# Who turns q and k, who applies the mask, and in what order: three changes at once to a BigBird attention and Fourier-mixing kernel

## The chip, the cores and the metric

The kernel runs on one NeuronCore of a Trainium2 chip. Times are device microseconds (us) of that core, from the first instruction to the last; "ns" is written where nanoseconds are meant. The profile of a kernel is one of its executions, so its span can differ from the median by a few tenths of a per cent.

## The reference, cut to what matters

```python
# attention: batch 4, 8 heads, 768 positions, 64 features a head, blocks of 32 positions
scores = scale * np.matmul(q, k.transpose(0, 1, 3, 2))
mask = np.abs(blk_i - blk_j) <= 1                      # a window of blocks,
mask = mask | (blk_i == 0) | (blk_j == 0) | (blk_i == 23) | (blk_j == 23)   # the outer blocks,
...                                                    # and three random blocks a row
scores = np.where(mask, scores, -1e9)
attn = softmax(scores);  x = attn @ v                  # heads side by side: 768 x 512 a batch
# Fourier mixing and channels
u  = x + real(fft(fft(x, axis=1), axis=2))
un = (u - mean(u)) / np.sqrt(var(u) + 1e-6)
out = u + np.maximum(un @ w_ch1, 0) @ w_ch2            # 512 -> 2048 -> 512
```

All of it is fp32. The output must agree with the reference.

Of the kernel before, what the change touches and what calls it, by code (L numbers as in the profile page):

```python
# [11 lines left out]
FP32 = mybir.dt.float32  # L12
BF16 = mybir.dt.bfloat16
# [4 lines left out]
ALU = mybir.AluOpType  # L18
ACT = mybir.ActivationFunctionType
# [45 lines left out]
           ((384, 64, 191, 64, 64, -1), (704, -128, 64, 63, 63, -1), (640, 127, 0, 1, 1, 1)))  # L65


def _rows(view, tile):

    got = []  # L70
    for t, p0, runs, jump, n, s0, step in _ORDER:
        if t != tile:
            continue
        at = view[s0:s0 + 1, :]
        row, col = list(at.ap[0])[0], list(at.ap[1])
        if jump > 0:
            got.append((p0, runs * n, bass.AP(tensor=at.tensor, offset=at.offset,
                                              ap=[[jump * row, runs], [step * row, n], col])))
            continue
        for r in range(runs):  # L80
            at = view[s0 + r * jump:s0 + r * jump + 1, :]
            got.append((p0 + r * n, n, bass.AP(tensor=at.tensor, offset=at.offset,
                                               ap=[[step * row, n], col])))
    return got
# [3 lines left out]
def kernel(  # L88
# [32 lines left out]
    scale = 1.0 / float(D) ** 0.5  # L121
    KA = D + NB
    NP = H // 2
    LIMIT = 400.0

    const = ctx.enter_context(tc.tile_pool(name="const", bufs=1))

# [49 lines left out]
    def busy(engine, us, after=0.0):  # L177
        when[engine] = max(when[engine], after) + us
        return when[engine]
# [13 lines left out]
    pairs = [(b, j) for b in range(B) for j in range(NP)]  # L193
    loaded, v_of = {}, {}

    def load_k(n, queue=None):

        b, j = pairs[n]
        kt = loaded.get((n, 1))
        if kt is None:  # L200
            kt = ld.tile([P, C, 2, D], FP32, tag="k", name="kr")
        for i in range(2):
            (queue or nc.sync).dma_start(out=kt[:, :, i, :],
                                         in_=k[b, 2 * j + i].rearrange("(p c) d -> p c d", p=P))
        loaded[n, 1] = kt

    def load_q(n):

        b, j = pairs[n]
        qt = loaded.get((n, 0))  # L210
        if qt is None:
            qt = loaded[n, 0] = ld.tile([P, T, 2, 2, D], FP32, tag="q", name="qr")
        for t in range(T):
            for i in range(2):
                rows = q[b, 2 * j + i][2 * P * t:2 * P * (t + 1), :]
                nc.sync.dma_start(out=qt[:, t, :, i, :],
                                  in_=rows.rearrange("(p r) d -> p r d", r=2))
# [47 lines left out]
    def warm(n):  # L265

        m = ps_m.tile([P, P], FP32, tag="m", name="warm")
        for _ in range(n):
            nc.tensor.matmul(m, ident, ident, start=True, stop=True)
# [126 lines left out]
    def room(i, shape, name, dtype=FP32):  # L396
        return big.tile(shape, dtype, tag=f"big{i}", name=name)
# [29 lines left out]



    turned, e_of, acc_of, o_of, sums_of, x_of, sp_of = {}, {}, {}, {}, {}, {}, {}  # L430
    s_at, e_at, oT_at, acc_at = {}, {}, {}, {}

    def turn(n, a, half):

        t = loaded[n, a]
        if half == 0:
            turned[n, a] = tp_p.tile([P, S], FP32, tag="qk"[a] + "T", name="qk"[a] + "T")
        dst = turned[n, a]
        first = n == 0 and half == 0
        tag, pool = ("m", ps_m) if first and a == 0 else ("t", ps_t)  # L440
        tp, at = pool.tile([P, 512], FP32, tag=tag, name="tp"), bank(tag)
        if a == 0:
            parts = [t[:, c // 2, c % 2, :, :] for c in (range(4, 6) if half else range(4))]
        else:
            parts = [t[:, T * half + c, :, :] for c in range(T)]
        for c, part in enumerate(parts):
            nc.tensor.transpose(tp[:, c * P:(c + 1) * P], part, ident)  # L447
        done = busy("PE", 0.15 * len(parts)) + HOP
        if a == 1:
            nc.scalar.copy(out=dst[:, half * HS:(half + 1) * HS], in_=tp[:, 0:HS])  # L450
            give(at, busy("ACT", 0.5, done))
        else:
            for i, (to, to_jump, frm, jump, cnt, step) in enumerate(_TURNED[half]):
                on, copy = (("DVE", nc.vector.tensor_copy) if n == 0 and (half == 1 or i % 2 == 0)
                            else ("ACT", nc.scalar.copy))
                copy(out=_grid(dst, to, 2, to_jump, cnt, 1),
                     in_=_grid(tp, frm, 2, jump, cnt, step))
                end = busy(on, 0.27 if cnt > 1 else 0.18, done)
            give(at, end)
        if half == 1:  # L460
            flat = t.rearrange("p t r i d -> p (t r i d)" if a == 0 else "p c i d -> p (c i d)")
            nc.scalar.activation(out=flat, in_=flat, func=ACT.Square,
                                 accum_out=peaks[:, 2 * n + a:2 * n + a + 1])
            busy("ACT", 1.05)

    UP = 2 * C
    UNITS = len(pairs) * UP
    SLOT = 2

    def scores(u):  # L470
        n, w = divmod(u, UP)
        half, c = divmod(w, C)
        qT, kT = turned[n, 0], turned[n, 1]
        s = ps_s.tile([P, 2, 512], FP32, tag="s", name="s")
        busy("PE", 0.72 if n >= NP else 1.0, max(e_at.get(u - SLOT, 0.0), z_at[u % 2]))
        s_at[u] = when["PE"] + HOP
        for i in range(2):
            nc.tensor.matmul(s[:, i, 0:HS], kT[D * i:D * i + D, c * P:(c + 1) * P],  # L478
                             qT[D * i:D * i + D, half * HS:(half + 1) * HS],
                             start=True, stop=n >= NP)  # L480
        if n < NP:
            for i in range(2):
                nc.tensor.matmul(s[:, i, 0:HS], of_k[D * i:D * i + NB, c * P:(c + 1) * P],  # L483
                                 off_q[D * i:D * i + NB, half * HS:(half + 1) * HS],
                                 start=False, stop=True)
        return s

    def weigh(u, s):
        n, w = divmod(u, UP)
        half, c = divmod(w, C)  # L490
        e = ep.tile([P, 2, HS], FP32, tag="e", name="e")
        e_of[u] = e
        if n < NP:
            nc.scalar.activation(out=e, in_=s[:, :, 0:HS], func=ACT.Exp, scale=scale)
            e_at[u] = busy("ACT", 0.8, s_at[u]) + HOP
            return
        nc.scalar.activation(out=s[:, :, 0:HS], in_=s[:, :, 0:HS], func=ACT.Exp, scale=scale)  # L497
        m = mask[:, c, half * HS:(half + 1) * HS].rearrange("p (o s) -> p o s", o=1)
        nc.vector.tensor_tensor(out=e, in0=s[:, :, 0:HS], in1=m.broadcast_to([P, 2, HS]),  # L499
                                op=ALU.mult)  # L500
        e_at[u] = busy("DVE", 0.97, busy("ACT", 0.8, s_at[u]) + HOP) + HOP
        if c > 0:
            acc_at[n, half] = busy("POOL", 2.0, e_at[u]) + HOP
        if c == 1:
            acc_of[n, half] = acc_p.tile([P, 2, HS], FP32, tag="acc", name="acc")

        for i in range(2 if c > 0 else 0):
            acc = acc_of[n, half][:, i, :]
            nc.gpsimd.tensor_add(out=acc, in0=e_of[u - 1][:, i, :] if c == 1 else acc,  # L509
                                 in1=e[:, i, :])  # L510
# [646 lines left out]
    def begin(b):  # L1157


        before, after, rest = mixer(b, x_of[b, 0], x_of[b, 1])  # L1160
        any_of = len(late) + len(apart) + 4 * len(rest)
        hold = 2 * T
        apart.extend((*step, any_of) for step in norm_steps(b) + before)
        apart.extend((*step, hold) for step in after)
        apart.append(("-", lambda: late.extend(rest), 0.0, 0.0, 0.0, hold))

    def w_loads():
        while state["got"] < min(len(wchunks), state["w"] + ROOMS):
# [3 lines left out]
    def w_steps(sl):  # L1172
        while state["w"] < min(len(wchunks), W_PACE * sl):
            w_round(state["w"])
            state["w"] += 1

    def slot(sl):
# [35 lines left out]
            short.append(("t", acc_at[n - 1, 1], lambda: total(n - 1)))  # L1213
        if n + 1 < len(pairs):
            for at, a, half in ((1, 0, 0), (2, 0, 1), (4, 1, 0), (5, 1, 1)):
                if s == at:
                    short.append(("t", 0.0, lambda a=a, half=half: turn(n + 1, a, half)))
            if s == 1:
                load_v(n + 1)
# [15 lines left out]
            channel_step()  # L1235
            gap(max(state["owed"], 0.0))

        while short and (s in (2, 5) or len(short) > 1 or phase == 0 or sl == B * SB):
            short.popleft()[2]()
        if s == 3 and n + 2 < len(pairs):  # L1240
            load_q(n + 2)
        if s == 0 and 0 < n < len(pairs) - 1:
            load_k(n + 1)
        w_loads()
        w_steps(sl)
        if sl >= 4 and sl % 2 == 0:
            table_step()

# [20 lines left out]
    state["got"] = 2  # L1269
    turn(0, 1, 0)  # L1270
    turn(0, 0, 0)
    warm(3)
    spread_q(keep_q[0:NB, :], keep)
    w_loads()
    for sl in range(B * SB + 1):
# [112 lines left out]
```

## The kernel before: the parts that the change touches

Two heads make a pair, so there are 16 pairs in 4 batches. A **unit** is one block of 128 keys against half the queries (384), for the two heads of a pair: 12 units a pair, 192 in all. A **slot** is two units. In each slot TensorE makes the scores of two units, ScalarE exponentiates them, and TensorE multiplies the exponentials of the slot before with v. Around this, the generator deals out other work: Fourier mixing and channel products of earlier batches, and small tasks from a list called `short`. It places them by a model of its own, `when[engine]`, advanced by `busy(engine, us)`. The model decides the order in which instructions are written; the engines then work off their queues in that order.

The turn of q or k of a pair, in two halves each: six blocks of 128 x 128 are transposed on TensorE into PSUM, the memory that TensorE's products land in (here its bank `t`), and copied to `qT` or `kT` in SBUF, the core's working memory. q is copied into an order that suits the Fourier mixing, in several pieces:

```python
def turn(n, a, half):                       # pair n, a = 0 for q, 1 for k
    tp, at = pool.tile([P, 512], FP32, tag=tag, name="tp"), bank(tag)
    for c, part in enumerate(parts):
        nc.tensor.transpose(tp[:, c * P:(c + 1) * P], part, ident)
    if a == 1:
        nc.scalar.copy(out=dst[:, half * HS:(half + 1) * HS], in_=tp[:, 0:HS])
    else:
        for i, (to, to_jump, frm, jump, cnt, step) in enumerate(_TURNED[half]):
            on, copy = (("DVE", nc.vector.tensor_copy) if n == 0 and (half == 1 or i % 2 == 0)
                        else ("ACT", nc.scalar.copy))
            copy(out=_grid(dst, ...), in_=_grid(tp, ...))
    ...                                     # then ScalarE sums squares for a later check
```

The mask. In the first batch (`n < NP`, pairs 0 to 3) TensorE adds it to the scores as a product of two small bf16 factors, 24 rows deep. From the second batch on VectorE multiplies a 0/1 mask in after the exponential:

```python
def scores(u):
    for i in range(2):
        nc.tensor.matmul(s[:, i, 0:HS], kT[D*i:D*i+D, c*P:(c+1)*P], qT[...], start=True, stop=n >= NP)
    if n < NP:
        for i in range(2):
            nc.tensor.matmul(s[:, i, 0:HS], of_k[...], off_q[...], start=False, stop=True)

def weigh(u, s):
    if n < NP:
        nc.scalar.activation(out=e, in_=s[:, :, 0:HS], func=ACT.Exp, scale=scale)
        return
    nc.scalar.activation(out=s[:, :, 0:HS], in_=s[:, :, 0:HS], func=ACT.Exp, scale=scale)
    nc.vector.tensor_tensor(out=e, in0=s[:, :, 0:HS], in1=m.broadcast_to([P, 2, HS]), op=ALU.mult)
    ...                                     # GpSimd adds e to a running sum
```

The small tasks of a slot are taken strictly in the order in which they were listed. After them come the loads of weights and their rounding on ScalarE and VectorE (`w_steps`):

```python
        while short and (s in (2, 5) or len(short) > 1 or phase == 0 or sl == B * SB):
            short.popleft()[2]()
        ...
        w_loads()
        w_steps(sl)                         # five VectorE instructions for each of its weights
```

## Time and profile before

| | before |
|---|---|
| median of the runs taken with the changed kernel | 1109.45 us (1108.4 to 1109.5) |
| span of the profiled run | 1109.3 us |
| TensorE busy | 96% |
| VectorE busy | 60% |
| mean granted TensorE clock | 0.994 |
| stretches at half clock before the last product | 3, of 3.4 us each |

TensorE is the bound, so a microsecond is lost in one of three ways: TensorE has more to do, it waits, or it works at half clock. The clock falls to half in stretches: in this trace the granted clock is 0.50 for 3.4 us from 190.6, 248.6 and 282.8 us on, and such a stretch does 1.7 us of work. I cut the trace at three points of equal work: the first scores of unit 48 (the first of the second batch), the first scores of unit 158 (in pair 13, late in the attention) and the end. In the view of windows, the columns are the window, its length, then the busy time of TensorE, of its weight loads, of VectorE, ScalarE and GpSimd, the granted clock, the DMA share and GB/s. Before:

```profile
0.00:133.30 133.30, 124.96 (x767) 46.93 (x767) 104.87 (x248) 101.01 (x206) 3.68 (x14) 1.00 0.62 185
133.30:711.00 577.70, 557.04 (x2241) 273.47 (x2240) 345.35 (x566) 201.41 (x427) 209.32 (x218) 0.99 0.09 23
711.00:1109.30 398.30, 385.67 (x1442) 224.12 (x1441) 214.53 (x404) 91.69 (x185) 61.21 (x70) 1.00 0.06 16
```

TensorE is idle for 8.3, 20.7 and 12.6 us of the three; some of the last is the end of the program, where nothing is left to overlap.

### The profile page before, as it was taken

The page shows a single profiled execution, that of the slowest core. Times are in us where ns is not written, and L with a number is a line of the kernel's source. Part 1 is how long each engine was busy: PE and PEld are TensorE (multiplying, and loading weights), DVE is VectorE, ACT ScalarE, POOL GpSimd, SP SyncE. Part 2 cuts the span into 40 slices and gives each one's busy share as a digit, 9 for nine tenths or more (in the row PEclk, how much of TensorE's full clock was granted, in tenths as well). Part 3 has the DMA queues.
Part 4 walks back from the last instruction along what each step waited for, and adds up shares of the span by engine and source line. Part 5 has one row for each costly group of instructions (what it writes and reads, how often), then busy time and mean ns, then how long its engine had stood idle before and what let it go on. Part 6 is the DMA issues. An engine that isn't in the chain of part 4 may idle for free.

```text
span 1109.3 us, 12468 instructions
## 1 busy us (share of the span) xinstructions
PE 1067.7 (96%) x4446; PEld 544.5 (49%) x4446; DVE 664.8 (60%) x1216; ACT 394.1 (36%) x818; POOL 274.2 (25%) x302
## 2 busy tenths in 40 slices
PE   8999988998899999999999999999999999999996
PEld 3333333544455545444444555454444555568675
DVE  5888878497754525653459355544356446575563
ACT  6788755555212102353443212244330202120210
POOL 1000088688100001245537000344540000000000
PEclk9999999999999999999999999999999999999999
DMA  7756311011000000211110000111000000100001
GB/s 219 208 176 215 93 51 43 15 45 42 1 1 1 0 1 19 66 33 27 43 29 15 1 0 1 51 50 29 1 1 0 1 1 19 39 1 1 1 16 45
DMA packets 65187, 44.30 MB, mean 40 GB/s; under 512 B 52814, under 2 KB 57948, under 8 KB 65116
## 3 DMA queue, kind: packets, MB, share of 16 engines
q1 hardware_dynamic: 63228, 42.62, 13.7%
q10 hardware_dynamic: 1856, 0.79, 0.3%
q8 instruction: 37, 0.61, 0.2%
q14 instruction: 34, 0.28, 0.1%
q0 software_dynamic: 32, 0.01, 0.0%
HBM read 37.11 MB, written 6.29 MB: 39 GB/s over the span
## 4 chain that ended last, share of the span: by engine, by line
PE 85%; DVE 9%; ACT 2%; issue 2%; DMA 0%; POOL 0%; SPq 0%; ACTq 0%; DVEq 0%; POOLq 0%
PE y L954 23%; PE z L898 15%; PE s L478 10%; PE o L522 9%; PE yp L898 7%; PE yy L1017 6%; PE xp L898 4%; DVE e L499 2%; PE tp L447 2%; PE zp L711 1%; PE sp L569 1%; PE zp L682 1%; PE xt L540 1%; PE s L483 1%; PE utp L823 1%
## 5 line engine op out<-in xcount | busy, mean ns | idle before, releaser
L509 POOL TENSOR_TENSOR acc<-acc,e 128x384 f32<-128x384 f32 x192 | 198.3, 1066 | 90.6 <-DVE e L499 90.1
L499 DVE TENSOR_TENSOR e<-s,mask 128x768 f32<-128x768 f32 x144 | 131.2, 951 | 78.4 <-ACT s L497 78.0
L478 PE MATMUL s<-qT,kT 64*128 64x384 f32 x768 | 161.7, 526 | 8.5 <-DVE e L499 7.4
L522 PE MATMUL o<-e,vr 128*64 128x384 f32 x768 | 145.1, 499 | 0.0
L497 ACT ACTIVATE s<-s 128x768 f32<-128x768 f32 x144 | 109.3, 795 | 65.5 <-PE s L478 64.9
L957 DVE TENSOR_TENSOR x<-y,x 128x512 f32<-128x512 f32 x72 | 49.8, 691 | 133.9 <-PE y L954 133.8
L954 PE MATMUL y<-w_sb,hB 128*128 128x512 f32 x288 | 128.4, 595 | 1.1 <-DVE x L957 1.0
L954 PE MATMUL y<-w_sb,hA 128*128 128x512 f32 x288 | 128.8, 594 | 0.6 <-ACT zs L713 0.6
L509 POOL TENSOR_TENSOR acc<-e 128x384 f32<-128x384 f32 x48 | 51.8, 1100 | 231.3 <-DVE e L499 173.2
L903 DVE TENSOR_TENSOR hA<-z,hA 128x384 f32<-128x384 f32 x64 | 35.7, 558 | 111.4 <-PE z L898 111.4
L478 PEld LDWEIGHTS s<-qT,kT 64*128 64x128 f32 x768 | 63.1, 187 | 68.1 <-DVE e L499 25.3
L898 PE MATMUL z<-unT,t 128*128 128x384 f32 x256 | 93.0, 486 | 0.0
L774 POOL TENSOR_SCALAR st<-st 128x1 f32<-128x1 f32 x24 | 6.6, 276 | 344.5 <-DVE st L773 344.1
L954 PEld LDWEIGHTS y<-w_sb,hB 128*128 128x128 f32 x288 | 53.3, 190 | 64.7 <-issue 62.1
L522 PEld LDWEIGHTS o<-e,vr 128*64 128x64 f32 x768 | 46.6, 136 | 73.9 <-issue 71.4
L954 PEld LDWEIGHTS y<-w_sb,hA 128*128 128x128 f32 x288 | 52.9, 190 | 59.6 <-issue 56.6
L907 ACT ACTIVATE hA<-hA 128x384 f32<-128x384 f32 x64 | 33.5, 524 | 123.6 <-DVE hA L903 123.1
L898 PEld LDWEIGHTS z<-unT,t 128*128 128x128 f32 x256 | 48.6, 190 | 33.9
L907 ACT ACTIVATE hB<-hB 128x384 f32<-128x384 f32 x64 | 33.6, 525 | 85.6 <-DVE hB L903 85.6
L898 PE MATMUL z<-t,w_sb 128*128 128x384 f32 x128 | 48.0, 499 | 3.1 <-DVE t L860 3.1
L898 PE MATMUL xp<-unT,w_sb 128*128 128x384 f32 x128 | 47.1, 491 | 1.5 <-ACT zs L713 1.1
L898 PE MATMUL yp<-unT,w_sb 128*128 128x384 f32 x128 | 46.7, 488 | 0.2 <-DVE un L747 0.2
(190 smaller groups left out, 1395.1 us busy)
## 6 DMA issues: line engine op xcount, KB each, us to landing
wraw<-in_moe_w_ch_dram SPq DMA_DIRECT2D x32, 512.0 KB
qr<-in_q_dram SPq DMA_DIRECT2D x90, 64.0 KB
vr<-in_v_dram SPq DMA_DIRECT2D x30, 192.0 KB
kr<-in_k_dram SPq DMA_DIRECT2D x28, 192.0 KB
out_dram<-x SPq DMA_DIRECT2D x16, 128.0 KB
out_dram<-x SPq DMA_DIRECT2D x8, 256.0 KB
out_dram<-x SPq DMA_DIRECT2D x8, 126.0 KB
out_dram<-x SPq DMA_DIRECT2D x4, 252.0 KB
```

Source lines behind the costliest of these rows:

```text
L447: nc.tensor.transpose(tp[:, c * P:(c + 1) * P], part, ident)
L478: nc.tensor.matmul(s[:, i, 0:HS], kT[D * i:D * i + D, c * P:(c + 1) * P], qT[D * i:D * i + D, half * HS:(half + 1) * HS], start=True, stop ...
L497: nc.scalar.activation(out=s[:, :, 0:HS], in_=s[:, :, 0:HS], func=ACT.Exp, scale=scale)
L499: nc.vector.tensor_tensor(out=e, in0=s[:, :, 0:HS], in1=m.broadcast_to([P, 2, HS]), op=ALU.mult)
L509: nc.gpsimd.tensor_add(out=acc, in0=e_of[u - 1][:, i, :] if c == 1 else acc, in1=e[:, i, :])
L522: nc.tensor.matmul(o[D * i:D * i + D, :], vt[:, i, c, :], e[:, i, :], start=(c == 0), stop=(c == C - 1))
L898: nc.tensor.matmul(to, a[:, k, :], c[:, k, :], start=(k == 0), stop=(k == ND // 2 - 1))
L903: tt(out=to, in0=ps, in1=a, op=ALU.add)
L907: nc.scalar.activation(out=h, in_=h, func=ACT.Relu)
L954: nc.tensor.matmul(y, hs[0, half][:, l, m * P:(m + 1) * P], w2_sb[:, 4 * r + l, :], start=(l == 0), stop=(l == 3))
L957: nc.vector.tensor_tensor(out=x[:, m, :], in0=y, in1=x[:, m, :], op=ALU.add)
L1017: nc.tensor.matmul(ps, a[:, k, :], c[k // 2][:, k % 2, :] if isinstance(c, list) else c[:, k, :], start=(k == 0), stop=(k == 3))
```

## The change

It has three parts, made at once. **Turning**: for the last eight pairs (`BY_VECTOR = 2 * NP`), q and k are loaded in pieces of 32 x 32 and transposed on VectorE, in place. q is then brought into its order by six ScalarE copies in a row; k is not, and the scores read its columns as weights with a step. **Masks**: in the second batch TensorE goes on applying the mask until channel products begin. The two bf16 factors lie where later data will go, so they are first copied elsewhere by four DMAs. **Order**: a small task whose inputs or bank are not ready, by the model, is passed over. Of the first q, ScalarE makes copies that VectorE made, and more warming products (of an identity matrix, with results that nobody reads) fill the start.

```diff
+    BY_VECTOR = 2 * NP
+    def load_blocks(n, a, tile): ...      # four DMAs, runs of 128 bytes
+    def keep_factors():
+        kept = room(2, [P, 2, S], "factors", BF16)
+        for a, t in enumerate(factors["at"]):
+            for rows in (slice(0, NB), slice(D, D + NB)):
+                nc.sync.dma_start(out=kept[rows, a, :], in_=t[rows, :])
+        factors["at"] = kept[:, 0, :], kept[:, 1, :]
 ...
-                on, copy = (("DVE", nc.vector.tensor_copy) if n == 0 and (half == 1 or i % 2 == 0)
+                on, copy = (("DVE", nc.vector.tensor_copy) if n == 0 and half == 1
 ...
+    def flip_blocks(n, a):
+        nc.vector.transpose(out=t, in_=t)
+    def in_order(n):
+        for to, frm, *dims in _IN_ORDER:  # six copies
+            nc.scalar.copy(out=_at(qT, to, ...), in_=_at(t, frm, ...))
 ...
+        if n < NP or (factors["at"]):
+            by_pe.add(u)                  # this unit's mask on TensorE
-            nc.tensor.matmul(s[:, i, 0:HS], kT[D * i:D * i + D, c * P:(c + 1) * P],
+            nc.tensor.matmul(s[:, i, 0:HS],
+                             _run(keys, c, P, C) if n >= BY_VECTOR else keys[:, c * P:(c + 1) * P],
 ...
+        if u in by_pe:
+            at_k, at_q = factors["at"]
 ...
-        while short and (s in (2, 5) or len(short) > 1 or phase == 0 or sl == B * SB):
-            short.popleft()[2]()
+        while short and (s in (2, 5) or len(short) > 1 or phase == 0 or r == 0):
+            ready = [i for i in short if max(i[1], min(free[i[0]])) <= when["PE"] + 0.1]
+            if not ready and s not in (2, 5) and r > 0:
+                break
+            item = ready[0] if ready else short[0]
+            short.remove(item)
+            item[2]()
+        if BY_VECTOR <= n + 1 < len(pairs):
+            for at, fn, args in ((0, squares, (n + 1, 0)), (1, flip_blocks, (n + 1, 0)),
+                                 (2, in_order, (n + 1,)), (3, squares, (n + 1, 1)),
+                                 (4, flip_blocks, (n + 1, 1))):
+                if s == at: fn(*args)
         w_loads()
         w_steps(sl)
+        if sl == SB - 3:
+            keep_factors()
 ...
-    warm(3)
+    warm(7)
```

(A limit of the later check also went from 400 to 200; it moves no work.)

## The prediction

> **What bounds the kernel now.** I read the page's first two parts, then the busy time of each engine in four stretches that I cut by stage (first batch's attention; second batch's; attention of batches three and four among the channel work; the last channels), then the TensorE waits of the second stretch, then the order of time.
>
> ```profile
> PE 1067.7 (96%) x4446; PEld 544.5 (49%) x4446; DVE 664.8 (60%) x1216; ACT 394.1 (36%) x818; POOL 274.2 (25%) x302
> ...
> 0.00:138.00 138.00, 129.25 (x794) 48.57 (x794) 109.40 (x258) 104.57 (x213) 3.68 (x14) 1.00 0.61 182
> 138.00:290.00 152.00, 134.85 (x706) 61.33 (x707) 115.43 (x158) 79.52 (x172) 111.93 (x112) 0.97 0.15 37
> 290.00:830.00 540.00, 535.98 (x2000) 264.87 (x2000) 282.93 (x485) 165.32 (x342) 153.38 (x164) 1.00 0.07 19
> 830.00:1110.00 280.00, 267.59 (x949) 169.75 (x947) 157.00 (x319) 44.70 (x93) 5.22 (x12) 0.99 0.04 12
> ```
>
> Columns after the length: busy TensorE, weight loads, VectorE, ScalarE, GpSimd, granted clock. TensorE bounds nearly everything: from 290 to 830 us it is idle for 4 of 540 us, so there a TensorE instruction saved is time saved. The second stretch is different: 17 of 152 us idle, and a clock of 0.97, which is 0.03 x 152 = 4.6 us more. Its waits:
>
> ```profile
> PE s L478 <- DVE e L499: 7.2, 9, 2.2
> PE z L898 <- DVE t L860: 3.1, 1, 3.1
> PE tp L447 <- ACT qT L456: 2.2, 2, 1.1
> PE xt L540 <- DVE sums L551: 1.3, 1, 1.3
> PE utp L823 <- DVE un L786: 1.3, 1, 1.3
> PE xt L540 <- ACT oT L528: 1.3, 2, 0.6
> PE tp L447 <- issue: 0.9, 1, 0.9
> ```
>
> VectorE, which multiplies the mask in after the exponential (951 ns each) beside the Fourier mixing of batch one, holds back the scores and the channels.
>
> [...] the clock is lower only where the waits are (0.91 in three slices of 20 us, at 180, 240 and 280 us).[...] of the two lines below, the first is that cast, the second a copy as long that reads in sequence:
>
> ```profile
> L238 DVE CAST at_k<-wide x1: 833/833/833, 3.2 to 3.2; 24x768 bf16<-24x768 f32 x1
> ...
> L232 DVE COPY wide<-maskT x1: 541/541/541, 5.9 to 5.9; 24x768 f32<-24x768 f32 x1
> ```
>
> The cast may be slower for its type too.[...] two instructions of one form took 0.75 us, and 1.78 us beside GpSimd.[...] with the 691 ns that 512 elements take here[...], I estimate 0.95 us for 768.
>
> **The change part by part.** Counts are from the instruction order of both kernels, which is fixed when built.
>
> *Turning on VectorE (pairs 8 to 15).* It removes 96 of 192 TensorE transposes. In the order of time:
>
> ```profile
> 155.05 0.55 PE L447 MATMUL tp<-ident,kr 128*128 128x128 f32 x3
> 155.53 1.56 PE L478 MATMUL s<-qT,kT 64*128 64x384 f32 x8
> 157.02 1.51 PE L522 MATMUL o<-e,vr 128*64 128x384 f32 x8
> ...
> 170.14 0.66 PE L447 MATMUL tp<-ident,qr 128*128 128x128 f32 x4
> 170.73 1.51 PE L522 MATMUL o<-e,vr 128*64 128x384 f32 x8
> 172.17 0.44 PE L447 MATMUL tp<-ident,qr 128*128 128x128 f32 x2
> 172.54 1.56 PE L478 MATMUL s<-qT,kT 64*128 64x384 f32 x8
> ```
>
> From start to start: 0.48 twice for k, 0.59 and 0.37 for q: 1.92 us a pair, times 8 = **15.4 us off**, where TensorE is full. VectorE gains 16 transposes x 0.95 = 15 us, mostly where it is half busy (283 of 540 us). ScalarE loses nine small copies and two of k, gains six from SBUF: no bound. The loads go to runs of 128 bytes, issued three slots ahead at a DMA share under 0.1: hidden.
>
> But k is no longer in the scores' order: its weights are read in steps of 24 bytes. Today such a load takes 187 ns under matmuls 322 ns apart, so it is hidden except once at each change of kind.[...] a load takes about 294 ns, still under 322; only the first of each of 48 slots shows: 0.107 x 48 = 5 us. If it cost more than 322, the other three passes of a slot show too, some 20 us in all. Weighted (half nothing, four tenths 5, one tenth 20): **4 us on**.
>
> *Masks of batch two on TensorE.* The order shows 38 of 48 units moved (mask multiplies 144 to 106; the first channel product comes after unit 86, before it was 108).[...] With the mask product a unit takes 1.11 us (below: 129.52 to 130.63), so a slot 2.22; without, 1.49 (above: 155.53 to 157.02).
>
> ```profile
> 129.52 0.92 PE L478 MATMUL s<-qT,kT 64*128 64x384 f32 x4
> 130.36 0.34 PE L483 MATMUL s<-at_q,at_k 24*128 24x384 bf16 x2
> 130.63 1.51 PE L522 MATMUL o<-e,vr 128*64 128x384 f32 x8
> ```
>
> 0.73 x 19 slots = **13.9 us on**. In return VectorE loses 38 x 0.951 = 36 us in that stretch, and the scores wait for ScalarE alone. Of the 17.3 us idle I expect 7 to stay: ScalarE's copies still block,[...] and the last five slots before unit 108 are as before. **10 us off.** A stretch begun after a wait takes 1.78 for 1.56 us: ten fewer, **2 off**. Clock: 4.6 us, one drop may stay: **3 off**.
>
> *Order.* ScalarE alone copies the first q, seven warm matmuls fill the gap, and a short task whose input is not ready is passed over. In the first stretch TensorE waits 5.1 us for such things (2.8 for ScalarE's o copy, 1.1 and 0.9 for its q copies, 0.3 for x): **3 off**. In the last two batches one or two like them go, and new waits for the flips come: **1 on**, net.
>
> Sum: -15.4 + 4 + 13.9 - 10 - 2 - 3 - 3 + 1 = -14.5; 1109.45 - 14.5 = 1095. I lean 2 us lower, as free strided weights are the likeliest single case: **1093 us**.
>
> **The rivals.** (1) Weight loads with a stride become the scores' bound. For: the slow cast, and TensorE has no slack from 290 us on. Against: 187 ns under 322 leaves room for nearly doubling. It would make 1105 to 1110, the transposes' gain given back. (2) All waits go: second-stretch idle to 2 us, no clock drop, free strides: -15.4 + 13.9 - 15 - 3 - 4.6 - 4 = -28, 1081. For: VectorE is relieved just where it is waited for. Against: GpSimd's 112 us in the second stretch. (3) The mask trade nets nothing: TensorE pays 13.9 us surely, and waits move from VectorE to ScalarE or GpSimd; with the turning alone, 1109 - 15 + 4 + some 5 = 1103. (4) A flip or square waits for its load of small runs and stalls an in-order queue; some 10 us; the low DMA share speaks against it.
>
> **Range and chances.** The transposes' saving and the masks' cost are sure within 1 us each; the strides (0 to 20) and the idle won (5 to 23) carry the spread. Range 1080 to 1105. Faster by over 2% needs under 1087: free strides and nearly all waits gone, 0.3. Within 2%: 0.67. Slower: over 1131, which no rival reaches alone: 0.03.
>
> **What would show it.** Transposes of kr and qr down to 96; TensorE idle in the second stretch about 7 us and its waits on the mask multiply gone before channels begin; one low-clock slice or none; scores' weight loads of the last eight pairs at 187 ns (free) or near 294, and the slot of eight score matmuls still 1.49 us from start to start or near 1.6; VectorE transposes near 0.95 us. I am wrong if that slot takes over 1.8 us, if ScalarE waits for GpSimd's sums by more than 5 us, or if a wait on a load of q or k appears.

## The result, and the profile after

The changed kernel took **1115.54 us** (1115.45 to 1115.63, four runs), where 1093 was predicted and 1080 to 1105 was the range. A ratio here is the mean time of one kernel's runs over the mean of the other's in the same rounds, so it is not quite the ratio of the medians quoted. It is 1.0057 (95% interval 1.004 to 1.0075): within 2%, and slower. All outputs are right.

Cut at the same work as before (unit 48, unit 158, the end), the windows of the changed kernel are:

```profile
0.00:143.60 143.60, 132.49 (x777) 50.16 (x777) 104.44 (x246) 100.97 (x209) 3.69 (x14) 0.95 0.59 173
143.60:712.20 568.60, 560.76 (x2239) 278.37 (x2238) 313.31 (x537) 197.90 (x396) 208.60 (x218) 1.00 0.11 24
712.20:1113.90 401.70, 387.16 (x1422) 230.14 (x1421) 218.47 (x410) 90.73 (x176) 61.25 (x70) 0.99 0.06 16
```

The middle part became 9.1 us shorter; TensorE's idle time there fell from 20.7 to 7.8 us. But the first part, where the change should matter little, became 10.3 us **longer**: 2.8 us more idle, and a clock of 0.95, which is 7 us more of a span of 143.6. The last part lost 3.4 us. So the larger part of what was lost is lost in the first 144 us, ahead of nearly all of the traded work. The last part, where turning should have saved time, lost some too.

The view of waits, of TensorE, names two that the kernel before did not have, the first and the last of these lines; the one between them is the wait on the mask multiply, 7.4 us before (columns: total us, times, longest):

```profile
PE s L560 <- DMA factors<-at_q: 4.3, 2, 3.8
PE s L553 <- DVE e L576: 4.1, 4, 1.6
PE tp L496 <- issue: 4.0, 1, 4.0
```

**The wait near 25 us.** In order of time, the changed kernel (the number after the start is the busy time of the group; in brackets, the idle time before it):

```profile
24.61 0.69 DVE L458 TENSOR_TENSOR w_sb<-w_sb,wraw 128x512 f32<-128x512 f32 x1
25.22 0.55 DVE L505 COPY qT<-tp 128x128 f32<-128x128 f32 x3
...
25.87 0.66 PE L496 MATMUL tp<-ident,qk 128*128 128x128 f32 x2 [3.99 <-issue]
```

and before:

```profile
22.90 0.44 PE L447 MATMUL tp<-ident,qk 128*128 128x128 f32 x2
```

Same work, 3 us earlier and without a wait. TensorE's turn of q (`tp`) needs the PSUM bank that the turn before still holds, until VectorE's three copies of it (25.22) are done. These copies were once queued ahead of the ten rounding instructions of slot 1. Now their task is "not ready" in slot 1 by the model, is passed over, and so lands behind `w_steps`: VectorE first rounds weights (the line at 24.61 is the last of it) and TensorE waits for 4 us. "Issue" in the bracket means only that the profile names no releaser.

**The wait near 130 us.** The DMA queue's issues (SPq) and TensorE, in order of time:

```profile
122.46 3.82 SPq L252 DMA_DIRECT2D qr<-in_q_dram  x6
...
126.37 1.75 SPq L476 DMA_DIRECT2D factors<-at_k  x2
...
128.17 1.48 SPq L476 DMA_DIRECT2D factors<-at_q  x2
...
130.21 0.32 PE L560 MATMUL s<-factors 24*128 24x384 bf16 x1 [3.85 <-DMA factors<-at_q]
```

The factors are copied from slot 21 and used from the very next one, unit 44, while the originals are still good. The four copies are issued behind six loads of q, and TensorE waits 3.85 and then 0.47 us.

**Half clock behind both.** Windows that I laid on the stretches at half clock in the changed kernel, and on the 3.4 us ahead of the third:

```profile
25.20:32.00 6.80, 6.13 (x20) 2.21 (x22) 3.41 (x9) 3.93 (x9) 0.00 (x0) 0.50 0.58 146
131.00:137.80 6.80, 6.80 (x26) 2.08 (x25) 3.01 (x6) 2.06 (x3) 0.00 (x0) 0.50 0.01 2
738.50:741.90 3.40, 1.78 (x10) 1.04 (x8) 1.82 (x2) 3.14 (x6) 0.83 (x1) 1.00 0.73 119
742.00:745.40 3.40, 3.40 (x13) 1.26 (x11) 2.71 (x3) 0.85 (x2) 3.17 (x5) 0.50 0.02 2
```

With each of the two waits the clock is at half for 6.8 us. The first of these stretches begins 0.7 us before its wait ends, so TensorE works 6.1 us in it and loses 3.1; in the second it loses 3.4. So the two cost 4.0 + 4.3 + 3.1 + 3.4, some 15 us, by this reading. The three stretches that the kernel before had in its second stretch, at 190.6, 248.6 and 282.8 us, are gone.

**The last part.** The third stretch at half clock has a small wait ahead of it:

```profile
736.50 1.87 ACT L534 COPY qT<-qb 128x256 f32<-128x256 f32 x6
...
740.18 1.89 PE L553 MATMUL s<-qT,kT 64*128 64x384 f32 x8 [1.62 <-DVE e L576]
```

ScalarE's six copies of q come in one burst ahead of the two exponentials of the slot, and so VectorE's mask multiply and then TensorE's next scores are 1.62 us late.

**Strides and transposes.** The weight loads of the scores in the kernel before and then in the changed one (ns: least, median, greatest), and VectorE's transposes of q:

```profile
L478 PEld LDWEIGHTS s<-qT,kT x768: 182/186/334, 9.2 to 823.1; 64*128 64x128 f32 x192
```

```profile
L553 PEld LDWEIGHTS s<-qT,kT x768: 182/292/335, 9.3 to 827.4; 64*128 64x128 f32 x192
```

```profile
L524 DVE STREAM_TRANSPOSE qb<-qb x8: 921/970/974, 268.4 to 769.4; 128x768 f32<-128x768 f32 x8
```

The second line mixes 384 plain loads with the 384 strided ones of the last eight pairs. Those alone, from 310 us on, take 292/294/315 ns; the estimate was 294. For the transposes it was 0.95 us. From the starts in the trace I worked out what a slot's eight score matmuls take from the first to the instruction behind them: in the last 48 slots the median is 1.602 us against 1.491, and summed over the 48 the difference is 5.0 us.

### The profile page after: what moved, and what is told of

Same layout as the page of the kernel before. It is cut to its first block, busy times and chain, and to the rows that moved or that the text cites. A ratio compares the mean times of both kernels' runs of the same rounds, so it can differ in the third digit from the quotient of the medians.

```text
span 1113.9 us, 12348 instructions
## 1 busy us (share of the span) xinstructions
PE 1080.4 (97%) x4434; PEld 558.7 (50%) x4434; DVE 636.2 (57%) x1191; ACT 389.6 (35%) x781; POOL 273.5 (25%) x302
## 4 chain that ended last, share of the span: by engine, by line
PE 91%; DVE 5%; ACT 2%; issue 1%; DMA 0%; SPq 0%; POOL 0%; ACTq 0%; POOLq 0%; DVEq 0%
PE y L1033 23%; PE z L977 15%; PE s L553 12%; PE o L601 11%; PE yp L977 7%; PE yy L1096 6%; PE xp L977 4%; PE s L560 2%; PE zp L790 1%; PE sp L648 1%; PE xt L619 1%; PE tp L496 1%; PE utp L902 1%; PE sp L662 1%; PE zp L761 1%
## 5 line engine op out<-in xcount | busy, mean ns | idle before, releaser
L553 PE MATMUL s<-qT,kT 64*128 64x384 f32 x768 | 171.3, 546 | 4.1 <-DVE e L576 4.1
L601 PE MATMUL o<-e,vr 128*64 128x384 f32 x768 | 148.4, 508 | 0.0
L576 DVE TENSOR_TENSOR e<-s,mask 128x768 f32<-128x768 f32 x106 | 96.5, 951 | 57.3 <-ACT s L574 51.8
L574 ACT ACTIVATE s<-s 128x768 f32<-128x768 f32 x106 | 79.9, 788 | 96.6 <-PE s L553 96.3
L553 PEld LDWEIGHTS s<-qT,kT 64*128 64x128 f32 x768 | 82.5, 245 | 59.0 <-issue 33.6
L571 ACT ACTIVATE e<-s 128x768 f32<-128x768 f32 x86 | 67.8, 814 | 25.4 <-PE s L560 23.3
```

The costliest lines, as they stand in the source:

```text
L553: nc.tensor.matmul(s[:, i, 0:HS], _run(keys, c, P, C) if n >= BY_VECTOR else keys[:, c * P:(c + 1) * P], qT[D * i:D * i + D, half * HS:(ha ...
L601: nc.tensor.matmul(o[D * i:D * i + D, :], vt[:, i, c, :], e[:, i, :], start=(c == 0), stop=(c == C - 1))
```

## The experiments

The theory after reading the traces: two accidental waits in the first stretch cost some 15 us with the half clock behind them; without them the change would gain. The rival: the time lies in the traded work itself (strides, masks, groups that follow), and the two waits only stand where other waits would have stood. "Before" in these rounds had medians of 1109.5 to 1109.7 us in runs 1 to 8 and of 1112.3 and 1111.7 us in the rounds of runs 9 to 12; there I go by ratios, or by two runs of the same rounds.

### 1 to 3. Each stall off, then both

```diff
 first_slots_drained: nothing is passed over in the first two slots
-            if not ready and s not in (2, 5) and r > 0:
+            if not ready and s not in (2, 5) and r > 0 and sl > 1:
 own_factors_first: the originals serve the first batch to its end
-            at_k, at_q = factors["at"]
+            at_k, at_q = factors["at"] if n >= NP else (of_k, off_q)
 both_stalls_off: both edits
```

> Theory: of the changed kernel's 10.2 us lost before unit 48, one part is the stall of 4.0 us at 22 us (three q copies of VectorE stand behind ten weight-rounding instructions, because the short task was passed over in the second slot) and the half clock that followed it (6.8 us at half, 3.4 us lost). Draining short tasks in the first two slots takes it away: 1115.5 - 4.0 - 3.4 = 1108 us, and no half clock near 25 us. Rival: that time comes back because the transposes then wait for a ScalarE copy of 1.1 us as before: 1109 to 1110. Rival: the stall was not the loss (the strided weights were): 1115.

> Theory: units 44 to 47 already read the kept mask factors, whose copies were issued at 126.4 us and landed 3.9 us after TensorE wanted them; 4.3 us of wait and 3.4 us of half clock after it. Reading the first batch's own factors up to unit 47 gives the copies three slots to land: 1115.5 - 4.3 - 3.4 = 1108 us, no wait on a transfer of the factors. Rival: the copies land so late that unit 48 waits instead: 1111 to 1115.

> Theory: the two stalls add: 1115.5 - 7.4 - 7.7 = 1100 us, inside the predicted range; idle before unit 48 under 5 us and no half clock there. Rival (strided weight loads are the main loss): over 1108 us still.

Measured: 1107.51 us (ratio to before 0.9976, 0.9955 to 0.9996), 1106.54 us (0.9971, 0.9954 to 0.9987), and 1100.85 us (0.9912, 0.9895 to 0.9928). All three as expected. Against the changed kernel's 1115.54 the two edits are worth 8.0 and 9.0 us, and together 14.7: the 15 us that the reading gave. The rival falls. In the trace with both off, unit 48 starts at 130.09 us, 3.2 us earlier than before (133.33).

### 4. Turning alone

Masks and order as before the change; only the turning is left. (The clearing of the list at the first slot of each batch, `r == 0`, stayed.)

```diff
-        if n < NP or (factors["at"]):
+        if n < NP:
 (and: no keep_factors, the old loop over `short`, the old copies, warm(3))
```

> The kernel before with only the turning of pairs 8 to 15 by VectorE. Theory: 96 transposes off (13.4 us by the accounts of the two traces), strided weights on (5 us), ScalarE's burst of six q copies delays some masks (3 to 4 us with a clock drop): 1109.5 - 13.4 + 5 + 3.5 = 1104.5 us. Rival (strides take back all that the transposes gave): 1109 to 1112.

Measured: 1115.49 us (1110.99 to 1119.72; ratio 1.0061, 1.0038 to 1.0084). A miss: turning by itself does not gain but **loses** some 6 us. The spread is large, and the profiled run is the fastest one, so its trace shows only part. In that part TensorE's transposes cost 13.4 us less, by my sums of starts, but its waits on the mask multiply grew. Before, over the whole program, and then with turning alone:

```profile
PE s L478 <- DVE e L499: 7.4, 10, 2.2
```

```profile
PE s L553 <- DVE e L576: 13.1, 13, 2.0
```

### 5. k brought into order

Both stalls off, and k is loaded to another buffer, flipped, and copied by one ScalarE instruction into the scores' order, so no weight load is strided. The steps of turning also move: q is flipped a slot earlier and squared later.

```diff
+    def k_in_order(n):
+        kT = turned[n, 1] = tp_p.tile([P, S], FP32, tag="kT", name="kT")
+        nc.scalar.copy(out=kT.rearrange("p (c b) -> p c b", c=C),
+                       in_=loaded[n, 1].rearrange("p (b c) -> p c b", c=C))
-                             _run(keys, c, P, C) if n >= BY_VECTOR else keys[:, c * P:(c + 1) * P],
+                             keys[:, c * P:(c + 1) * P],
-            for at, fn, args in ((0, squares, (n + 1, 0)), (1, flip_blocks, (n + 1, 0)),
-                                 (2, in_order, (n + 1,)), (3, squares, (n + 1, 1)),
-                                 (4, flip_blocks, (n + 1, 1))):
+            for at, fn, args in ((0, flip_blocks, (n + 1, 0)), (1, in_order, (n + 1,)),
+                                 (2, squares, (n + 1, 0)), (3, flip_blocks, (n + 1, 1)),
+                                 (4, k_in_order, (n + 1,)), (5, squares, (n + 1, 1))):
```

> Both stalls off, and k of pairs 8 to 15 copied by ScalarE (one copy of 768 a pair) into the scores' order, so that the weight loads read in sequence again. Theory: the strides cost 0.11 us in each of 48 slots: weight loads back at 187 ns, the slot of eight score matmuls back at 1.49 us, 1100.85 - 5.3 = 1095.5 us, less whatever the longer ScalarE queue costs (0 to 2 us). Rival: the strides were hidden and 1100 to 1101 stays.

Measured: **1093.36 us** (1093.15 to 1093.68; ratio 0.9848, 0.9832 to 0.9865), 7.5 us under run 3. The score matmuls are 5.1 us cheaper by the sums of starts, their waits on the mask multiply came down to two of at most 0.8 us, and no stretch at half clock is left before the end. The edit moves two things at once, strides and the place of the burst, so the 5.1 us belong to the strides and the rest to the waits only as the trace shows it; no run divides them.

### 6. The burst of q copies in two halves

Run 5 with three of the six copies in each of two slots.

```diff
-            for at, fn, args in ((0, flip_blocks, (n + 1, 0)), (1, in_order, (n + 1,)),
-                                 (2, squares, (n + 1, 0)), (3, flip_blocks, (n + 1, 1)),
+            for at, fn, args in ((0, flip_blocks, (n + 1, 0)), (1, in_order, (n + 1, 0)),
+                                 (2, in_order, (n + 1, 1)), (3, squares, (n + 1, 0)),
+                                 (3, flip_blocks, (n + 1, 1)),
```

> As k_in_order, with ScalarE's six q copies dealt over two slots. Theory: the waits of scores on the mask multiply (1.6 us twice, 0.7 once, and one half clock of 1.7 us) come from the burst of 1.9 us on ScalarE ahead of the exponentials; halved it goes: another 3 to 5 us off, 1091 to 1093. Rival: those waits come from VectorE's own load: no change against k_in_order.

Measured: 1110.18 us (ratio 0.9995, 0.9978 to 1.0011), 17 us over run 5. A miss, and not by the bursts. ScalarE and TensorE in the order of time in this run:

```profile
716.76 0.48 ACT L627 COPY x<-xt 128x384 f32<-128x384 f32 x1 [12.35 <-DMA out_dram<-x]
...
719.87 2.93 PE L560 MATMUL s<-qT,kT 64*128 64x384 f32 x8 [11.43 <-DVE e L583]
```

ScalarE's copy of an attention result into `x` must wait until an earlier batch's output has been stored from that buffer. The generator wrote this copy earlier, presumably because of the other durations in its model: ahead of the q copies and of an exponential pair, behind which it stands in run 5. So it stood at the head of ScalarE's queue for 12 us, with the exponentials behind it, and the clock was at half for 10.2 us from 713.7 on. In run 5 the same copy starts at 716.47, after a wait of 0.6 us. The run says nothing about the bursts; it shows that a small edit that reorders a generated queue can cost more than what it was meant to test.

### 7. Both stalls off, without turning

```diff
-    BY_VECTOR = 2 * NP
+    BY_VECTOR = B * NP
```

> Both stalls off, masks and order kept, TensorE transposes all pairs again. Theory: the turning is worth 13.4 - 5.3 (strides) - 3.5 (ScalarE bursts) = 4.6 us here: 1105.5. Rival, since turning alone was not faster (1115.5 against 1109.5): the turning costs, and this is under 1099.

Measured: 1099.59 us (ratio 0.9904, 0.9887 to 0.992). A miss by 6 us, and the key one: with turning (run 3) 1100.85, without it 1099.59. As made, **turning is worth nothing**. By the sums of starts between the two traces, turning saves 13.0 us of transposes and gives back 6.3 us in the scores (5.0 of them strides, which go in run 5), 4.3 us in other groups (2.9 in `y`, `xp` and `utp`, which used to follow a transpose, and 1.4 in `o`, from a stretch at half clock at 728.3 us), and 4.3 us of idle time. With k in order (run 5) it is worth 6.2 us.

### 8. Masks alone

The kernel before with the masks of the second batch on TensorE, the original factors used to the end of the first batch; no turning, no new order.

```diff
-    BY_VECTOR = 2 * NP
+    BY_VECTOR = B * NP
-            at_k, at_q = factors["at"]
+            at_k, at_q = factors["at"] if n >= NP else (of_k, off_q)
 (and: the old loop over `short`, the old copies, warm(3))
```

> The kernel before with only the masks of batch two on TensorE, with the first batch's own factors to unit 47. Theory: 76 mask products and the split scores cost 11.6 us, and the idle of the second stretch (some 12 us), its half clocks (5 us) and restarts go: 1109.5 + 11.6 - 17 - 2 = 1102. Rival: the trade nets nothing: 1108 to 1111.

Measured: 1102.78 us (ratio 0.9934, 0.9917 to 0.995). As expected: the mask trade gains 6.9 us. In the 19 slots that changed, scores and mask products together take 42.4 us where the scores took 30.8, so 11.6 us more, and the idle time fell by 15.6 us, with all three half clocks gone. (The profiled run, at 1104.4 us the slowest of the four, has another one, of 3.4 us at 9.3 us, behind a wait for the first q.)

### 9. The order alone

The kernel before with the new loop, the copies of the first q and the warming products; no turning, masks as before.

> The kernel before with the new order alone: masks and turning undone. My reading: the three tasks of the first slots are now passed over until the ten weight-rounding instructions have gone to VectorE, so TensorE waits 4.0 us for bank t and runs some 3.4 us at half clock behind it; what the order change was meant to save, 3.2 us by the end of batch one, is there when that is taken away (both_stalls_off against before). So 1109.5 + 4.0 + 3.4 - 3.2 = 1113.5 us (1111.5 to 1115.5), with the wait of 4.0 us before the turn of q near 25 us. Rival: without the kept factors' work at hand the first stretch has other idle time and the stall hides in it; then 1106 to 1110.

Measured: 1117.69 us (1117.13 to 1118.53) where before had 1112.34 in the same rounds; ratio 1.0061 (1.0034 to 1.0087), so 6.8 us slower, and 4 were expected. The wait of 4.0 us is there. By unit 48 its trace is 2.4 us behind the kernel before; the further loss comes after, beginning with a wait of 1.51 us on the mask multiply where before had 0.48. Behind it the trace has a stretch at half clock at 151.4 us, which the kernel before does not have (1.7 us lost), and by unit 158 it is 5.8 us behind. What brings the longer waits about, no run shows.

### 10. Turning alone, with k in order

Run 4 with the edit of run 5.

> The run turning_alone (masks and order undone, 1115.5 us with a wide spread) with k also brought into the scores' order by one ScalarE copy, so that no weight load of the scores is strided. If the strides and the waits behind ScalarE's burst are what made turning cost instead of gain, it is now worth what it was worth between stalls_off_no_turning and k_in_order, 6 us: 1103.5 us (1101 to 1106), the weight loads of the scores back at 187 ns, and the waits of the scores for the mask multiply below 8 us. Rival: turning_alone was slow for another reason, the old order of channel work or DMA waits at 278 us, which k in order does not touch; then 1108 to 1112.

Measured: 1109.56 us (1107.27 to 1110.63), before 1112.34; ratio 0.9981 (0.9952 to 1.001), a gain of 2 us that the interval does not secure. A miss of my own reading, which gave 6, though the strides and the burst did explain most of run 4: k in order moved the ratio from 1.0061 to 0.9981, some 9 us. The waits on the mask multiply stayed at 11.0 us, and the idle time is 6.2 us above before. The larger part of that stands at one place, from 271 to 279 us, where the first channel products of batch one begin: TensorE's transposes of the normalised rows (`utp`) wait 5.9 us on VectorE, against 1.3 before, and the clock is at half for 10.2 us from 273.3 on, against 3.4 before. By my reading VectorE waits there for a small step of GpSimd (`un` on `st`), which stands behind GpSimd's running sums; the changed kernel has three such waits, 12.1 us in all. Run 4 shows the same: 4.5 us, and 6.8 us at half clock. So where VectorE still has all the masks of the second batch, turning comes with waits that it does not bring in run 5; which of its instructions causes them, no run shows. That makes the parts dependent on each other: turning is worth about 2 us alone and 6 with the mask trade and the order.

### 11 and 12. The order, without its stall

Run 5 with the old order of small tasks, the old copies and warm(3); and run 5 again, in the same rounds.

> k_in_order (1093.4 us) with the order of the kernel before in the first slots: the three small tasks are taken as they come, 3 warming products and the old split of the copies. My reading: with its stall taken away the new order saves the 3.2 us that it saved by the end of batch one in both_stalls_off, and nothing else; so 1093.4 + 3.2 = 1096.6 us (1095 to 1099), with unit 48 some 3 us later than in k_in_order and no wait of 4 us near 25 us. Rival: order_alone, which lost 6 us where the stall explains only some 4, says that the new order is worth nothing or less at all; then 1090 to 1094 us.

> The same kernel as k_in_order, on the chip and in the rounds of the run with the old order, so that their difference is read on one chip: 1093.4 us (1091.5 to 1096).

Measured: 1097.26 us (ratio 0.9888, 0.9856 to 0.992) and 1093.30 us (ratio 0.9840, 0.982 to 0.986). As expected: with its stall taken away, the new order is worth 4.0 us by the medians; in the traces 4.1 us of it are there by unit 48. Run 12 repeats run 5: 1.6% under the kernel before, the best version found.

## Why the prediction was wrong, point by point

The groups of the prediction's sum, against the runs (differences of medians, us; a plus is slower):

| group | predicted | measured | from |
|---|---|---|---|
| masks: 13.9 - 10 - 2 - 3 | -1.1 | -6.9 | run 8 against its before |
| order | -3 | -4.0 | run 12 against run 11 |
| turning: -15.4 + 4 + 1 | -10.4 | +1.3 | run 3 against run 7 |
| the wait near 25 us, with its half clock | not in the sum | +8.0 | after against run 1 |
| the wait near 130 us, with its half clock | not in the sum | +9.0 | after against run 2 |

The first three make -9.6, so 1100, where run 3 measured 1100.85; the two stalls together add 14.7 (run 3 against after), which makes 1115. The account closes within 1 us, but the groups are not independent (runs 9 and 10), so this is how they stand in this kernel. That run 3 falls inside the range is partly luck: turning came out 11.7 us worse than predicted, masks and order together 6.8 us better.

1. **The step that failed** is "3 off" for the order, "In the first stretch TensorE waits 5.1 us for such things". The saving was right, but the step asked only which waits the new order removes, never which it makes. A task passed over does not vanish: it moves behind what its slot issues afterwards, here ten instructions on VectorE. And the copy of the factors has no term at all: its place in the DMA queue and its first use, one slot apart, stood in the diff. Without the two, the change took 1100.85 us (run 3), inside the range.

2. **"15.4 us off"** for the transposes was mis-sized. It took one pair's durations, 1.92 us, from the attention of the second batch, where the groups stand ahead of score and value products. Most of the removed ones stand beside channel work. In the kernel before, of the second half of k and both halves of q:

```profile
566.42 0.55 PE L447 MATMUL tp<-ident,kr 128*128 128x128 f32 x3
566.80 1.46 PE L898 MATMUL xp<-unT,w_sb 128*128 128x384 f32 x4
...
587.23 0.66 PE L447 MATMUL tp<-ident,qr 128*128 128x128 f32 x4
587.73 3.60 PE L954 MATMUL y<-w_sb,hA 128*128 128x512 f32 x8
...
591.16 0.38 PE L447 MATMUL tp<-ident,qr 128*128 128x128 f32 x2
591.47 1.56 PE L478 MATMUL s<-qT,kT 64*128 64x384 f32 x8
```

   From start to start 0.38, 0.50 and 0.31, and 0.48 for the first half of k: 1.67 us, times 8 = 13.4, which is what run 4's trace saved. And part of that returns: the group behind a removed transpose now starts behind another kind of work. A `y` group takes 3.43 us to the next start behind a transpose (587.73 above), and 3.63 behind a value product (594.40 to 598.03). In run 5 against run 7, where neither strides nor a half clock blur it, 4.2 us came back: `y` 1.7, scores 1.2, `xp` 0.8, `utp` 0.4, `o` 0.1. The prediction had no term for it.

3. **"4 us on"** for the strides was right in kind and size: a strided load of 294 ns, as estimated, and 5.0 us in the slots. "Hidden except once" holds (0.104 us in each of the 48 slots, where one load got 0.108 us longer), and rival 1, strides as the scores' bound, is refuted. Two grounds were weaker than they looked: the 294 ns was my estimate, with no trace behind it then, and the copy set beside the slow cast does not read in sequence, it reads each of 24 numbers 32 times.

4. **"1 on, net"** for new waits of the flips was mis-sized. The prediction counted ScalarE's copies as "no bound" by their sum. By the traces what counted was that six come at once ahead of two exponentials: a wait of 1.62 us, and a half clock behind it. In run 3 against run 7 idle time is 4.3 us higher. This, the strides and point 2 are why turning is worth nothing as made; that the burst causes these waits is read from the order of time alone, since run 6, made to test it, could not.

5. **Masks**: the cost was right. It was put at 13.9 us, less 2 for restarts, and is 11.6 (run 8; an undisturbed slot takes 2.23 us for 1.49). The gain was mis-sized: 13 (10 of idle, 3 of clock), where it is 18.5, the cost and the net gain of 6.9 together. "Second-stretch idle to 7" was too careful: from 138 to 290 us the changed kernel's TensorE is idle for 2.3 us of 152. Rival 3, that the trade nets nothing, is refuted.

6. **Clock**: in the stretch where it was expected all three drops went, worth 5.1 us where 3 were counted. Two longer ones appeared in the first stretch, out of the stalls. "Only where the waits are" holds in the prediction's own trace, but TensorE did not stand still before the three drops: it was busy for 1.5, 1.5 and 0.5 of the 3.4 us ahead of them.

7. **Rival 2** (all waits go) came true only for the second stretch. **Rival 4**, a flip that waits for its load and stalls a queue, did not show in the changed kernel. Run 6 showed its mechanism at another place: a store, ScalarE's queue, 12 us.

What stays open: why turning alone varied between 1111 and 1120 us, why the order alone (run 9) loses more time after unit 48, and what the bursts cost by themselves.

## What to carry to other kernels

When a change reorders work, list for every instruction that moves later who holds what it frees, and what it now stands behind in its engine's queue: the passed-over copy kept a PSUM bank for 4 us because rounding of weights stood ahead of it. A copy that only makes room must be issued well before its first use, or be used only when the original really goes. And a wait of TensorE is to be counted with the half clock behind it: here the two of 4.0 and 4.3 us cost 8.0 and 9.0.

## What the traces show of the hardware

- Half clock. The traces of the kernel before and of the changed one have six drops before the last products. The granted clock is 0.50 in each, for 3.4 us in four and for 6.8 us in the two by the waits of 4.0 and 4.3 us. TensorE was busy for 0.08 to 1.78 us of the 3.4 us ahead of each; ahead of the drop at 742 us it was 1.78 us, with one wait, of 1.62 us. That little work does not always bring a drop: in the kernel before TensorE was busy for 1.41 us of the 3.4 from 144.8 us on, and the clock was 1.00 in the 3.4 us behind. What sets a drop off, no run shows.
- Weight loads. Here 128 columns took 91 ns in bf16 (the mask factors) and, in fp32, 141 ns in the transposes and 186 ns in the scores; with a step of 24 bytes the scores' took 294 ns, 108 more, about 0.84 ns a column. What the step costs is measured; why, no run shows.
- VectorE's transpose of 128 x 768 fp32 in 32 x 32 blocks took 0.97 us. The 0.95 us was an estimate; the mask multiply of 128 x 768 in the kernel before took 0.951 us.
- VectorE beside GpSimd. In the kernel before, two instructions of line 761 (128 x 255) took 0.75 us from 214.19 us on, while GpSimd was idle, and 1.78 us from 216.75 us on, beside GpSimd's running sums. What lengthened them, no run shows.
- What follows a removed TensorE transpose got dearer: 4.2 us came back here (run 5 against run 7) for 96 transposes (13.1 us) taken away. That it comes from the change of one kind of product to another is my reading.
